# Refitting a list scheduler: measured latencies, GpSimd durations and the shared port, with new priorities

## The chip, the cores and the metric

The kernel runs on one core of a Trainium2 chip. The time is the device time of one execution in microseconds (us). The core has four engines that compute (PE, the TensorE that multiplies matrices; DVE, the VectorE; ACT, the ScalarE; POOL, the GpSimd) and SP, which issues most transfers. Each engine takes its instructions strictly in the order in which the program lists them: an instruction that waits holds up all that stand behind it on the same engine.

## The reference

Three layers follow each other. The first is a complex linear recurrence for 4 batches of 8 heads, 768 steps, head size 48; the second a gated feed-forward layer with a three-tap convolution over time; the third a causal attention with four experts, of which each token takes two. Cut to what matters:

```python
# layer 1: complex decay a (length limited to 0.999), state S, output y
for t in range(S):
    S_re, S_im = ar * S_re - ai * S_im + kv, ar * S_im + ai * S_re   # kv = outer(k[t], v[t])
    y[:, :, t] = einsum('bhd,bhde->bhe', q[:, :, t], S_re)
# layer 2
h = maximum(x @ w_in, 0); conv = sum_k conv_w[k] * shift(h, k)
x = (h * sigmoid(conv)) @ w_out
# layer 3, for each of 4 experts e
a = softmax(causal((x @ wq[e]) @ (x @ wk[e]).T / 8))
out += gate[e] * (a @ (x @ wv[e])) @ wo[e]                           # gate: the two best of x @ w_gate
```

## The kernel before

Stage 1 replaces the recurrence by sums over chunks of 128 steps. The decays are turned to logarithm and angle (`polar`, `phase` in `e_ops`, with Ln, Exp, Arctan and Sin on ACT and elementwise work on DVE), summed along time by a matmul with a triangle (L437), and multiplied onto q and k (`rotate`; the products go through `Ctx.mul`, L394). `e_ops` does this for 12 units of 256 tokens, three to a batch. `m_ops` then does 24 chunks of 128 tokens: the scores of a chunk (PE L585), their causal mask (DVE L587), the state (PE L605, DVE L614), the output (PE L623 and L627), its copy to SBUF (ACT L633) and, for each unit, a store to the buffer `x_scr` in DRAM.

Stage 2 (`s2_ops`) takes 8 blocks of 384 tokens. A block loads its `x` from `x_scr`, splits it into a rounded part and a rest (`Ctx.cp`, a cast, L384 on ACT or L386 on DVE; then a subtraction, L394), multiplies by `w_in` (PE L762, nine matmuls a slice of 128 features), applies Relu (ACT L773), the convolution (DVE L784, 16 of them a block), Tanh (ACT L786) and the gate (DVE L787), and multiplies by `w_out` (PE L800). The weights are unpacked on the way from 64-bit words (`weights`, L684 to L694). Stage 3 (`s3_ops`) is the attention: projections (PE L870, L920), scores (PE L1017, L1018; DVE L1026; ACT L1029), transposes (PE L1042), the product with v (L977) and the last projection (L998), then the store to `out`.

None of this is written in the order in which it runs. Every step is entered in a list with what it reads and writes, the engines that may do it (`alts`: an engine and an assumed duration for each) and a priority. `Sched.run` then plays a list scheduler: it goes through assumed time, gives each free engine the ready step of the smallest priority number, chooses between engines by who would end first, places the tiles in memory, and `emit` writes the instructions in the order of assumed start times. So assumed durations and latencies decide the order of instructions, which engine takes a step, and nothing else: the program still waits for real data by semaphores. Three things in the model are touched by the change:

- Latencies: `Sched.LAT` is what passes from the end of a step to the start of one that needs it on another engine.
- The port that DVE and POOL share: a step is in `lock` if it runs on POOL, or on DVE without touching PSUM and without `alone=True`; two locked steps never overlap in assumed time.
- Durations: `pool(n)` for an elementwise step of n columns on POOL, `dve(n)` and `acts(n)` for DVE and ACT, and single numbers.

The dictionary `P` holds the offsets of all priorities, some buffer counts and thresholds. The assumed time of a transfer is not changed: it starts 0.65 us after its issue or when the one before it is through, moves 360 kB a microsecond, and is there 1.1 us later.

Where the scheduler foresees a gap on PE in the early part, it fills it with small matmuls on a constant tile (L641, `heat`, up to the first block of stage 2; L645, `warmth`, in foreseen gaps of over 0.6 us after that). They compute nothing that is used.

Of the kernel before, what the change touches and what calls it, by code (L numbers as in the profile page):

```python
# [14 lines left out]
AF = mybir.ActivationFunctionType  # L15
# [21 lines left out]
TWO_PI = 6.28318501  # L37
TINY64 = 1.125 * 2.0 ** -15
P = dict(tu=22.99, lag=1.78, tf=3.56, dn=29.40, pa=28.16, pf=31.65, pp=31.74, ps=19.16, pr=13.53, kn=9.56, pd=-10.31,
         py=-3.49, cw=7.07, cs=6.91, ne=3, sw=16.78, slack=0.33, hold=1.18, wl=0.23, bl=0.07, bc=0.37, hy=7.06,  # L40
         tb=28.68, xp=-21.85, jq=-1.43, jp=3.08, jv=-4.00, ja=-2.43, jf=16.61, jt=5.79, ju=0.10, jw=0.26, na=13, no=2,
         nt=6, ns=4, nx=7, nq=14, th=0.46, fr=0.20, nc=2, sd=1, ck=-587.37, up=61.76, big=0, a0=1, a1=4, u0=-0.59,
         u1=0.11, u2=3.11, u3=-0.41, u4=0.75, u5=1.55, u6=-0.26, u7=1.62, u8=0.57, u9=-4.01, u10=-7.57, u11=-0.52,
         v0=-0.57, v1=-0.88, v2=2.18, v3=0.15, v4=1.22, v5=1.18, v6=0.00, v7=-7.38, v8=-7.08, v9=-5.79, v10=3.04,
         v11=-7.00, b0=0.00, b1=-4.24, b2=-0.23, b3=7.87, b4=-0.60, b5=-0.53, b6=-3.32, b7=-1.95, b8=-2.61, c0=0.89,
         c1=-2.69, c2=1.81, c3=-0.52, pw=0.14, sp=1.00, jg=-4.92, pm=-1.39)
# [48 lines left out]
class Sched:  # L95
    LAT = {"PE": 0.32, "ACT": 0.2, "DVE": 0.2, "POOL": 0.22, "SP": 0.05}
# [63 lines left out]
    def run(self):  # L160
# [37 lines left out]
        while done < total:  # L198
# [95 lines left out]
            for s in o.out:  # L294
                s.nd -= 1
                lat = 0.06 if s.alts.keys() == {e} else self.LAT["SP" if "SP" in o.alts else e] + (0.22 if "PE" in s.alts else 0.0)
# [41 lines left out]
def acts(n):  # L338
    return 0.095 + n * 0.000834


def dve(n, fast=False):
    return 0.066 + n * (0.00052 if fast else 0.00104)


def pool(n):
    return 0.1 + n * 0.0019
# [56 lines left out]
def s1_ops(c):  # L404
# [10 lines left out]
    def e_ops(u):  # L415
# [23 lines left out]
        def polar(z, a, b):  # L439
# [16 lines left out]
                r=ks(im), w=ks(tmp), prio=pa, alone=True))  # L456
# [4 lines left out]
            S.op({"ACT": acts(N)}, lambda e: A.activation(g(tmp), g(re), AF.Exp, bias=c.cs["b_eps"], scale=-1.0),  # L461
# [14 lines left out]
        def phase(z, a, b):  # L476
# [44 lines left out]
            S.op({"ACT": acts(N)}, lambda e: A.activation(f(n), f(n), AF.Sin, scale=-TWO_PI, bias=c.cs["b_half"]),  # L521
# [46 lines left out]
    def m_ops(j):  # L568
# [60 lines left out]
        S.op({"PE": 2.07 if cc else 1.0}, f, r=[v, qp] + sm + ([s0] if cc else []), w=[ps], prio=d - P["py"])  # L629
# [41 lines left out]
def weights(c, src, cols, prio, early=False):  # L671
# [5 lines left out]
    else:  # L677
# [10 lines left out]
        S.op({"DVE": dve(cols, True), "POOL": pool(cols)}, lambda e: c.E[e].tensor_scalar(  # L688
# [571 lines left out]
```

## Time and profile before

| | us |
|---|---|
| median of 3 runs | 684.7 |
| lowest, highest run | 682.49, 687.74 |
| the profiled execution, its own time | 688.02 |
| its span, first to last instruction | 686.2 |
| PE, DVE, ACT, POOL busy | 643.2, 563.5, 482.9, 117.0 |
| mean granted TensorE clock | 0.989 of full speed |

The profiled execution is 3.3 us over the median of the runs. An engine is busy while one of its instructions runs, also when that instruction is held up inside by another engine. PEld is PE's loading of weights, which overlaps its matmuls. In the rows below, x26 is a number of instructions; behind a bar stand the busy time, the mean duration in ns, and the idle time of the engine before them with what ended it.

### The profile page before, as it was taken

To read this page: it belongs to the slowest core of one execution; us is meant where nothing else is said; L and a number is where in the kernel's file an instruction comes from. 1 tells how busy PE (TensorE), PEld (TensorE's weight loads), DVE (VectorE), ACT (ScalarE), POOL (GpSimd) and SP (SyncE) were. 2 spreads that over 40 slices of the span, in tenths; PEclk is the share of its full clock that TensorE was granted. 3 is DMA by queue.
4 is the path that set the end of the run, shared out by engine and by line. 5 is a ranking of instruction groups with operands and counts; after the bars stand their busy time and mean duration, and the time that the engine had idled before them with its cause. 6 is when DMAs were issued, how large, how long until landed. Compare 5 with 4: busy or idle time off the path is not lost. (4 is left out here: it accounts for less than half of the span.)

```text
span 686.2 us, 13132 instructions
## 1 busy us (share of the span) xinstructions
PE 643.2 (94%) x4724; PEld 574.3 (84%) x4724; DVE 563.5 (82%) x1235; ACT 482.9 (70%) x1007; POOL 117.0 (17%) x157
## 2 busy tenths in 40 slices
PE   6899698799999999999999999999989999999995
PEld 3568497799898899999999999996878889788874
DVE  5999799999989999989748998689687676876761
ACT  7968786788998977886427556469567745865762
POOL 0733120331242411102002000002111100100100
PEclk9999989999999999999999999999999999999998
DMA  8666857656647376455032231021011001000102
GB/s 310 162 201 187 229 155 219 189 174 205 169 158 222 102 225 188 128 154 162 24 114 83 71 105 57 1 70 36 1 36 69 36 1 68 4 1 1 47 25 75
DMA packets 54604, 76.58 MB, mean 112 GB/s; under 512 B 5104, under 2 KB 45936, under 8 KB 54528
## 3 DMA queue, kind: packets, MB, share of 16 engines
q1 hardware_dynamic: 54240, 75.04, 35.8%
q8 instruction: 39, 0.64, 0.4%
q0 software_dynamic: 288, 0.59, 0.3%
q14 instruction: 37, 0.30, 0.1%
HBM read 42.51 MB, written 14.16 MB: 83 GB/s over the span
## 5 line engine op out<-in xcount | busy, mean ns | idle before, releaser
L762 PE MATMUL banks<-arena_R 128*128 128x384 f32 (+1 forms) x472 | 103.8, 349 | 5.4 <-ACT arena_R L384 3.6
L800 PE MATMUL banks<-arena_R 128*128 128x384 f32 (+1 forms) x510 | 104.3, 344 | 0.0
L762 PEld LDWEIGHTS banks<-arena_R 128*128 128x128 f32 x472 | 84.8, 194 | 7.4 <-ACT arena_R L384 4.0
L800 PEld LDWEIGHTS banks<-arena_R 128*128 128x128 f32 x510 | 88.2, 188 | 2.0 <-issue 1.3
L384 ACT ACTIVATE arena_F<-banks 128x384 f32<-128x384 f32 (+4 forms) x146 | 61.4, 447 | 34.3 <-PE banks L1042 12.3
L784 DVE SCALAR_TENSOR_TENSOR arena_F<-arena_F 128x386 f32<-128x386 f32 (+1 forms) x128 | 77.6, 627 | 3.9 <-ACT arena_F L781 3.1
L384 ACT ACTIVATE arena_R<-arena_F 128x384 fp32r<-128x384 f32 (+2 forms) x85 | 44.6, 534 | 51.4 <-PE banks L800 20.6
L1029 ACT ACTIVATE arena_F<-arena_F 128x128 f32<-128x128 f32 (+5 forms) x96 | 63.5, 664 | 7.7 <-DVE arena_F L1026 7.0
L394 DVE TENSOR_TENSOR arena_R<-arena_F,arena_R 128x384 fp32r<-128x384 f32 (+1 forms) x86 | 56.6, 675 | 13.2 <-PE banks L800 10.0
L394 POOL TENSOR_TENSOR arena_F<-arena_F 128x768 f32<-128x768 f32 x26 | 50.5, 1946 | 93.4 <-issue 22.6
L1026 DVE CUSTOM_DVE_ANT_0 arena_F<-banks,cover 128x128 f32<-128x128 f32 (+5 forms) x96 | 56.9, 617 | 7.9 <-PE banks L1018 6.1
L394 DVE TENSOR_TENSOR arena_F<-arena_F 128x768 f32<-128x768 f32 (+1 forms) x65 | 60.9, 951 | 0.8 <-ACT arena_F L451 0.5
L358 ACT ACT_TABLE_LOAD x40 | 51.3, 1283 | 1.4 <-PEq L1252 0.8
L1042 PE MATMUL banks<-ident,arena_F 128*128 128x128 f32 x336 | 49.3, 275 | 2.5 <-DVE arena_F L386 2.1
L773 ACT ACTIVATE arena_F<-banks 128x384 f32<-128x384 f32 (+1 forms) x64 | 31.1, 487 | 25.7 <-PE banks L762 20.8
L1042 PEld LDWEIGHTS banks<-ident,arena_F 128*128 128x128 f32 x336 | 39.2, 141 | 7.7 <-DVE arena_F L386 2.5
L394 POOL TENSOR_TENSOR arena_R<-arena_F,arena_R 128x384 fp32r<-128x384 f32 (+1 forms) x18 | 20.2, 1122 | 127.8 <-ACT arena_R L384 120.0
L386 DVE COPY arena_F<-banks 128x512 f32<-128x512 f32 (+4 forms) x74 | 36.8, 517 | 4.4 <-PE banks L1042 2.1
L1017 PE MATMUL banks<-arena_R 128*128 128x384 f32 (+4 forms) x112 | 39.2, 359 | 1.2 <-ACT arena_F L384 1.0
L977 PE MATMUL banks<-arena_F 128*64 128x384 f32 (+2 forms) x288 | 39.7, 420 | 0.3 <-ACT arena_F L384 0.3
L787 DVE SCALAR_TENSOR_TENSOR arena_F<-arena_F 128x384 f32<-128x384 f32 (+1 forms) x64 | 36.2, 585 | 3.8 <-ACT arena_F L786 3.4
L623 PE MATMUL banks<-arena_Z 128*64 128x128 f32 x384 | 36.7, 278 | 0.8 <-ACT arena_R L384 0.8
(242 smaller groups left out, 1467.9 us busy)
## 6 DMA issues: line engine op xcount, KB each, us to landing
arena_F<-x_scr SPq DMA_DIRECT2D x12, 576.0 KB, 4.4
arena_Z<-v SPq DMA_DIRECT2D x12, 512.0 KB, 4.3
arena_C<-arena_F SPq DMA_DIRECT2D x36, 129.0 KB, 2.5
arena_F<-q SPq DMA_DIRECT2D x12, 384.0 KB, 4.0
arena_F<-k SPq DMA_DIRECT2D x12, 384.0 KB, 5.0
arena_B<-arena_F SPq DMA_DIRECT2D x36, 128.0 KB, 2.5
x_scr<-arena_Z SPq DMA_DIRECT2D x24, 192.0 KB, 3.3
out<-arena_F SPq DMA_DIRECT2D x24, 192.0 KB, 1.9
```

The costliest lines, as they stand in the source:

```text
L358: nc.scalar.preload_act_table_set(TABS[o.tab])
L384: self.A.activation(out(), in_(), AF.Copy)
L386: self.V.tensor_copy(out(), in_())
L394: self.E[e].tensor_tensor(out(), a(), b(), op=self.OPS[op])
L762: PE.matmul(ps.ap, wi[f][a][:, i * 128:(i + 1) * 128], x[i].ap, start=(n == 0), stop=(n == 8))
L784: S.op({"DVE": dve(no) + 0.06}, lambda e, i=i: V.scalar_tensor_tensor(cv.ap, h[:, i:i + no], cw[:, k3 + i:k3 + i + 1], cv.ap, op0=OP.mult, ...
L800: PE.matmul(o[:, i, :], a[:, m * 128:(m + 1) * 128], g_.ap, start=(f == 0 and n == 0 and len(g) == 1), stop=(f == FT - 1 and n == 2 and i ...
L977: PE.matmul(py[64 * r:64 * r + 64, :n], v[kb][:, o:o + HD], at[r][:, kb, :n], start=(kb == 0), stop=(kb == nk - 1))
L1017: PE.matmul(pp, q[:, qs], k[:, kk], start=True, stop=False)
L1026: S.op({"DVE": dve(n)}, lambda e: V.tensor_tensor_reduce(wide(a.ap), ps[:, :, :step], wide(c.cs["cover"][:, SEQ - n:]), 1.0, 3e38, op0=OP. ...
L1029: S.op({"ACT": acts(n) + 0.15}, lambda e: A.activation(a.ap, a.ap, AF.Exp, bias=nm.ap, scale=-1.0, accum_out=rs[:, at, r:r + 1]), r=[nm], ...
L1042: PE.transpose(pt[:, z, :], a[:, (g_ + z) * 128:(g_ + z + 1) * 128], ident)
```

## The change

No computation is added or dropped. The scheduler's model gets other numbers, and the priorities in `P` are fitted anew (41 of its entries differ; two lines stand for all). The minimum in `weights` (L688) may no longer run on POOL. The squares in `polar` (L454) are now counted as holding the shared port.

```diff
-P = dict(tu=22.99, lag=1.78, tf=3.56, dn=29.40, pa=28.16, pf=31.65, pp=31.74, ps=19.16, pr=13.53, kn=9.56, pd=-10.31,
+P = dict(tu=22.99, lag=1.78, tf=3.56, dn=28.53, pa=28.16, pf=31.65, pp=31.74, ps=19.16, pr=13.53, kn=10.80,
...
-    LAT = {"PE": 0.32, "ACT": 0.2, "DVE": 0.2, "POOL": 0.22, "SP": 0.05}
+    LAT = {"PE": 0.22, "ACT": 0.16, "DVE": 0.13, "POOL": 0.13, "SP": 0.05}
...
-                lat = 0.06 if s.alts.keys() == {e} else self.LAT["SP" if "SP" in o.alts else e] + (0.22 if "PE" in s.alts else 0.0)
+                lat = 0.0 if e == "PE" and "PE" in s.alts else self.LAT["SP" if "SP" in o.alts else e] + (0.1 if "PE" in s.alts else 0.0)
...
 def pool(n):
-    return 0.1 + n * 0.0019
+    return 0.19 + n * 0.00178 + (0.28 if n == 768 else 0.0)
...
                 g(tmp), g(im), g(im), 1.0, 0.0, op0=OP.mult, op1=OP.max, accum_out=okin[:, hi:hi + 1]),
-                r=ks(im), w=ks(tmp), prio=pa, alone=True))
+                r=ks(im), w=ks(tmp), prio=pa))
...
-            S.op({"ACT": acts(N)}, lambda e: A.activation(g(tmp), g(re), AF.Exp, bias=c.cs["b_eps"], scale=-1.0),
+            S.op({"ACT": acts(N) + 0.09}, lambda e: A.activation(g(tmp), g(re), AF.Exp, bias=c.cs["b_eps"], scale=-1.0),
...
-        S.op({"PE": 2.07 if cc else 1.0}, f, r=[v, qp] + sm + ([s0] if cc else []), w=[ps], prio=d - P["py"])
+        S.op({"PE": 1.9 if cc else 1.0}, f, r=[v, qp] + sm + ([s0] if cc else []), w=[ps], prio=d - P["py"])
...
-        S.op({"DVE": dve(cols, True), "POOL": pool(cols)}, lambda e: c.E[e].tensor_scalar(
+        S.op({"DVE": dve(cols, True)}, lambda e: V.tensor_scalar(
             t.ap.bitcast(F32), t.ap.bitcast(F32), TINY64, None, op0=OP.max), w=[t], prio=prio)
...
-        S.op({"PE": 0.66 * (nk - 2) + 0.69}, av, r=at + v[:nk], w=[py], prio=d + P["ja"])
+        S.op({"PE": 0.65 * (nk - 2) + 0.78}, av, r=at + v[:nk], w=[py], prio=d + P["ja"])
...
-        pd = 2 * (n // step) * (max(0.108, step / 2400) + 0.013)
+        pd = 2 * (n // step) * (max(0.108, step / 2400) + 0.013) + 0.06 * (nb - 1)
...
-        S.op({"ACT": acts(n) + 0.15}, lambda e: A.activation(
+        S.op({"ACT": acts(n) + 0.18}, lambda e: A.activation(
```

Line numbers of the changed kernel are one higher than those of the kernel before from L47 on (L394 is L395 there). The order is different nearly everywhere. Three places of it follow; `arena_F` and the like are the SBUF regions in which the tiles lie, `banks` is PSUM.

On POOL, its first work in stage 1, before:

```order
L688 TENSOR_SCALAR arena_F<-arena_F 128x384
L400 DMA arena_A_246<-arena_F 16x8x128 x2
L400 DMA arena_B_269<-arena_F 16x8x128 x3
L400 DMA arena_A_246<-arena_F 16x8x130 x2
L400 DMA arena_B_269<-arena_F 16x8x128 x2
L688 TENSOR_SCALAR arena_F<-arena_F 128x384 x3
L394 TENSOR_TENSOR arena_F<-arena_F 128x3x256
L688 TENSOR_SCALAR arena_F<-arena_F 128x384
L388 TENSOR_SCALAR arena_R<-arena_F 128x384
L394 TENSOR_TENSOR arena_Z_109<-arena_Z_109,arena_A_246 96x384
L394 TENSOR_TENSOR arena_F<-arena_F 128x768
L394 TENSOR_TENSOR arena_Z_109<-arena_Z_109,arena_C_449 96x384
```

The same place now:

```order
L401 DMA arena_A_253<-arena_F 16x8x128 x2
L401 DMA arena_B_276<-arena_F 16x8x128 x3
L401 DMA arena_A_253<-arena_F 16x8x130 x2
L401 DMA arena_B_276<-arena_F 16x8x128 x2
L389 TENSOR_SCALAR arena_R<-arena_F 128x384
L395 TENSOR_TENSOR arena_R<-arena_F,arena_R 128x384
L395 TENSOR_TENSOR arena_F<-arena_F 128x3x256
L395 TENSOR_TENSOR arena_F<-arena_F 128x768
L395 TENSOR_TENSOR arena_Z_109<-arena_Z_109,arena_C_454 96x384
```

The five L688 steps and most products of 96x384 (the state of a chunk times its decay) have left POOL for DVE. Over the whole program POOL loses 5 of 5 L688, 6 of 7 products of 96x384, 6 of 26 products of 128x768, and 6 of 19 subtractions of 384 and 386 columns; DVE issues 32 instructions more in all.

On SP, the transfers ahead of the first load of `x` (the row `arena_F<-x_scr`), before:

```order
L400 DMA arena_F<-w_in 128x768
L400 DMA arena_Z_109<-v 128x1024
L400 DMA arena_F<-a_im 128x768
L400 DMA x_scr<-arena_Z_109 48x4x256 x2
L400 DMA arena_F<-a_re 128x768
L400 DMA arena_F<-w_out 128x768
L400 DMA arena_F<-x_scr 128x3x384
L400 DMA arena_A_246<-arena_F 16x8x258 x6
L400 DMA arena_B_269<-arena_F 16x8x256 x6
```

The same place now:

```order
L401 DMA arena_F<-w_out 128x768
L401 DMA arena_F<-a_im 128x768
L401 DMA x_scr<-arena_Z_109 48x4x256 x2
L401 DMA arena_Z_109<-v 128x1024
L401 DMA arena_F<-x_scr 128x3x384
L401 DMA arena_F<-w_in 128x768
L401 DMA arena_F<-a_re 128x768
L401 DMA arena_A_253<-arena_F 16x8x258 x5
L401 DMA arena_F<-w_out 128x768
L401 DMA arena_A_253<-arena_F 16x8x258
```

One load instead of two stands between the store of the needed chunks and the load of `x`; three of the loads ahead of the store have gone behind.

On DVE, the last instructions ahead of the first cast of that `x`, before:

```order
L394 TENSOR_TENSOR arena_F<-arena_F 128x768
L394 TENSOR_TENSOR arena_R<-arena_F,arena_R 128x384
L394 TENSOR_TENSOR arena_F<-arena_F 128x3x256
L454 ISA arena_F,okin<-arena_F 128x768
L454 ISA okin 128x1
L447 TENSOR_SCALAR arena_F,okin<-arena_F 128x768
L394 TENSOR_TENSOR arena_F<-arena_F 128x768
L386 CAST arena_R<-arena_F 128x384
L394 TENSOR_TENSOR arena_R<-arena_F,arena_R 128x384 x3
```

The same place now:

```order
L460 SCALAR_TENSOR_TENSOR arena_F<-arena_F 128x768
L695 SCALAR_TENSOR_TENSOR arena_F<-arena_F 128x384
L395 TENSOR_TENSOR arena_Z_109<-arena_Z_109,arena_C_454 96x384
L387 CAST arena_R<-arena_F 128x384
L464 SCALAR_TENSOR_TENSOR arena_F<-arena_F 128x768
L395 TENSOR_TENSOR arena_R<-arena_F,arena_R 128x384
L395 TENSOR_TENSOR arena_F<-arena_F 128x768
L387 CAST arena_R<-arena_F 128x384 x2
L395 TENSOR_TENSOR arena_R<-arena_F,arena_R 128x384 x2
L387 CAST arena_R<-arena_F 128x384
```

All three casts of this `x` are now on DVE (before, two of them were on ACT). From the eighth L587, the mask of the last chunk that this `x` needs, to the first of these casts the program lists 26 rows on DVE before and 18 now. On PE, the L641 fillers go from 132 to 129 matmuls, the L645 fillers from 6 to 27; all other matmuls are the same in number. ACT has 42 table loads instead of 40.

## Rows read from the trace of the kernel before

**Rows 1.** The page: busy us and share of each engine.
```profile
PE 643.2 (94%) x4724; PEld 574.3 (84%) x4724; DVE 563.5 (82%) x1235; ACT 482.9 (70%) x1007; POOL 117.0 (17%) x157
```

**Rows 2.** Stretches: length, busy of PE, PEld, DVE, ACT, POOL, clock, DMA share, GB/s.
```profile
0.00:150.00 150.00, 127.04 (x1000) 101.41 (x1001) 133.44 (x276) 116.69 (x211) 42.17 (x44) 0.97 0.69 209
150.00:325.00 175.00, 170.50 (x1420) 163.18 (x1419) 164.77 (x282) 145.87 (x265) 41.56 (x54) 1.00 0.56 168
325.00:450.00 125.00, 124.74 (x806) 122.76 (x805) 100.26 (x191) 67.80 (x138) 9.07 (x33) 1.00 0.21 64
450.00:686.00 236.00, 220.95 (x1504) 186.94 (x1503) 165.04 (x489) 152.51 (x396) 24.24 (x26) 0.99 0.10 33
```

**Rows 3.** POOL's groups by line and shape, whole span.
```profile
L394 POOL TENSOR_TENSOR arena_F<-arena_F 128x768 f32<-128x768 f32 x26 | 50.5, 1946 | 93.4 <-issue 22.6 <-ACT arena_F L472 20.6 <-DVE arena_F L394 19.3
L688 POOL TENSOR_SCALAR arena_F<-arena_F 128x384 f32<-128x384 f32 x5 | 9.8, 1959 | 20.6 <-ACT arena_F L684 20.6
L394 POOL TENSOR_TENSOR arena_Z<-arena_Z,arena_C 96x384 f32<-96x384 f32 x4 | 3.7, 921 | 0.0
```

**Rows 4.** DVE's groups that read two SBUF tiles, 0 to 150 us.
```profile
L394 DVE TENSOR_TENSOR arena_F<-arena_F 128x768 f32<-128x768 f32 x22 | 24.5, 1125 | 0.0
L394 DVE TENSOR_TENSOR arena_R<-arena_F,arena_R 128x384 fp32r<-128x384 f32 x23 | 13.9, 620 | 0.2 <-ACT arena_R L384 0.2
L454 DVE CUSTOM_DVE_ANT_0 arena_F<-arena_F 128x768 f32<-128x768 f32 x6 | 7.4, 1234 | 0.0
```

**Rows 5.** The same kinds, 150 to 325 us.
```profile
L394 DVE TENSOR_TENSOR arena_F<-arena_F 128x768 f32<-128x768 f32 x29 | 28.8, 1005 | 0.5 <-ACT arena_F L451 0.5
L394 DVE TENSOR_TENSOR arena_R<-arena_F,arena_R 128x384 fp32r<-128x384 f32 x18 | 15.0, 853 | 0.1
L394 DVE TENSOR_TENSOR arena_R<-arena_F,arena_R 128x386 fp32r<-128x386 f32 x16 | 11.4, 719 | 2.2 <-PE banks L800 2.2
```

**Rows 6.** Single lines on DVE: shortest, median and longest of one, in ns.
```profile
L394 DVE TENSOR_TENSOR arena_R<-arena_F,arena_R x86: 540/552/2195, 20.7 to 670.5; 128x384 fp32r<-128x384 f32 x54, 128x386 fp32r<-128x386 f32 x30, 128x768 fp32r<-128x768 f32 x2
L394 DVE TENSOR_TENSOR arena_F<-arena_F x65: 539/947/2579, 5.1 to 314.4; 128x768 f32<-128x768 f32 x51, 128x384 f32<-128x384 f32 x14
L454 DVE CUSTOM_DVE_ANT_0 arena_F<-arena_F x13: 558/951/1996, 5.7 to 270.1; 128x768 f32<-128x768 f32 x11, 128x384 f32<-128x384 f32 x2
L587 DVE TENSOR_TENSOR arena_Z<-banks,tri x48: 669/680/693, 32.8 to 348.8; 128x512 f32<-128x512 f32 x48
L688 DVE TENSOR_SCALAR arena_F<-arena_F x12: 171/351/364, 15.0 to 149.4; 128x384 f32<-128x384 f32 x11, 128x24 f32<-128x24 f32 x1
```

**Rows 7.** SP in order of time: start us, us of issuing, transfer.
```profile
70.18 0.83 SPq L400 DMA_DIRECT2D x_scr<-arena_Z  x2
...
75.97 0.39 SPq L400 DMA_DIRECT2D arena_F<-x_scr  x1
```

**Rows 8.** DVE in order of time: start us, us, instruction, idle before.
```profile
64.56 0.68 DVE L587 TENSOR_TENSOR arena_Z<-banks,tri 128x512 f32<-128x512 f32 x1
...
79.00 1.69 DVE L394 TENSOR_TENSOR arena_F<-arena_F 128x768 f32<-128x768 f32 x1
84.69 0.36 DVE L386 CAST arena_R<-arena_F 128x384 fp32r<-128x384 f32 x1 [3.99 <-DMA arena_F<-x_scr]
```

**Rows 9.** ACT, the copy of the last chunk that the first block needs.
```profile
69.52 0.63 ACT L633 ACTIVATE arena_Z<-banks 128x512 f32<-128x512 f32 x1
```

**Rows 10.** The page's transfers: number, KB each, median us from issue to landing.
```profile
arena_F<-x_scr SPq DMA_DIRECT2D x12, 576.0 KB, 4.4
...
x_scr<-arena_Z SPq DMA_DIRECT2D x24, 192.0 KB, 3.3
```

**Rows 11.** PE alone in two stretches: busy us, granted clock, DMA share, GB/s.
```profile
82.00:92.00 10.00, 6.74 (x27) 0.66 0.58 129
136.00:144.00 8.00, 6.18 (x45) 0.79 1.00 311
```

**Rows 12.** DVE in order of time: the start of the fifth block's convolution.
```profile
316.21 1.27 DVE L784 SCALAR_TENSOR_TENSOR arena_F<-arena_F 128x384 f32<-128x384 f32 x2
```

More of the change, by code (lines that the diff above doesn't have):

```diff
@@ L38 @@
 TINY64 = 1.125 * 2.0 ** -15
-P = dict(tu=22.99, lag=1.78, tf=3.56, dn=29.40, pa=28.16, pf=31.65, pp=31.74, ps=19.16, pr=13.53, kn=9.56, pd=-10.31,
[L40 to L46, printed above, removed]
+P = dict(tu=22.99, lag=1.78, tf=3.56, dn=28.53, pa=28.16, pf=31.65, pp=31.74, ps=19.16, pr=13.53, kn=10.80,
+         pd=-10.31, py=-3.58, cw=7.07, cs=6.91, ne=3, sw=18.37, slack=0.33, hold=0.93, wl=0.23, bl=0.06,
+         bc=0.37, hy=8.95, tb=28.68, xp=-21.94, jq=-1.05, jp=3.17, jv=0.63, ja=1.91, jf=16.96, jt=4.48, ju=0.10,
+         jw=0.26, na=15, no=2, nt=6, ns=4, nx=9, nq=14, th=0.39, fr=0.20, nc=2, sd=1, ck=-584.75, up=61.76,
+         big=0, a0=3, a1=4, u0=-2.06, u1=0.11, u2=3.11, u3=-0.41, u4=0.75, u5=1.83, u6=-0.10, u7=1.62, u8=0.57,
+         u9=-4.01, u10=-7.21, u11=-0.08, v0=-0.43, v1=-0.88, v2=1.92, v3=0.15, v4=1.22, v5=1.55, v6=0.33,
+         v7=-7.48, v8=-9.19, v9=-11.52, v10=3.04, v11=-7.00, b0=-0.47, b1=-4.24, b2=-0.23, b3=7.87, b4=-0.55,
+         b5=-0.97, b6=-3.68, b7=-1.53, b8=-2.61, c0=0.72, c1=-2.89, c2=2.35, c3=-0.35, pw=0.14, sp=1.00,
+         jg=-4.92, pm=-1.39)
 TABS = {"E": "natural_log_exp_and_others", "T": "trig_and_small", "S": "sigmoid_and_others",
@@ L520, in phase @@
             S.op({"ACT": acts(N), "DVE": dve(N, True)}, mag, r=ks(w), w=ks(n), prio=pp_)
-            S.op({"ACT": acts(N)}, lambda e: A.activation(f(n), f(n), AF.Sin, scale=-TWO_PI, bias=c.cs["b_half"]),
+            S.op({"ACT": acts(N) + 0.09}, lambda e: A.activation(f(n), f(n), AF.Sin, scale=-TWO_PI, bias=c.cs["b_half"]),
                  w=ks(n), prio=psn, tab="TU", grp=u)
@@ L958, in group @@
              alone=True)
-        S.op({"DVE": 0.3, "POOL": 0.5}, lambda e: (V if e == "DVE" else G).tensor_copy(
+        S.op({"DVE": 0.3, "POOL": 0.51}, lambda e: (V if e == "DVE" else G).tensor_copy(
             gx.ap, gs[:, :, :, None].to_broadcast([128, 3, 2, HD])), r=[gs], w=[gx], prio=d + P["jg"])
```

## The prediction

> **What bounds the kernel now.** I read the page first. PE is busy for 643.2 of 686.2 us, DVE for 563.5, ACT for 482.9, POOL for 117.0 [rows 1]. Since that is an average over three stages, the busy time by stretches comes next [rows 2]. The reader is to see two regimes there. Up to 325 us DVE is nearly always busy (133.44 of 150, then 164.77 of 175) while PE in the first 150 us is busy for only 127.04, part of which are fillers. From 150 us on PE has hardly a gap: 170.50 of 175, 124.74 of 125, 220.95 of 236, and part of the last difference is the tail in which the last results are stored. PE's computing work is the same before and after. So the time can fall only as far as PE gets more of it done in the first 150 to 250 us, where DVE feeds it, or stands less later; a gain that DVE makes after that is lost on a full PE.
>
> Then I looked at what makes DVE slow where it bounds. The product of 128x768 takes 947 ns in the median but up to 2579, the subtraction 552 but up to 2195, and the squares of L454 951 but up to 1996; the mask L587, which reads PSUM, stays between 669 and 693 [rows 6]. The first three read two SBUF tiles, and are held up inside while POOL works. Last I looked at where all engines stand at once: the first load of `x`. DVE waits 3.99 us for it [rows 8], and around it the granted clock of PE is 0.66 in the mean over 10 us, that is part of it on the lower level of 1.2 GHz, after PE had stood; there is a second such dip, 0.79 over 8 us, at 136 to 144 us [rows 11].
>
> **The change, part by part.** The sum is made against the profiled execution's 688.0 us, 3.3 over the median of 684.7; I carry the difference over to the median unchanged.
>
> *POOL gives work to DVE.* The order moves 6 products of 128x768, 6 of 96x384 and 5 minima L688 to DVE. At 0.947, 0.55 (the median of the 384-column subtraction, the nearest row) and 0.351 us [rows 6] that is 5.7 + 3.3 + 1.8 = 10.8 us more on DVE; another 13 casts come from ACT, at 0.35 (the L688 row, as near in size) 4.6 us. The rest of what changes on DVE cancels within about 3. Where does it fall? I took each order up to the 65th L784, the first one of the fifth block, at 316.21 us in the trace [rows 12]: DVE lists 531 instructions ahead of it before, 529 now. So the 15 us lie behind it, where DVE is busy for 100.26 of 125 us under a full PE [rows 2]. Cost 0; if that cover were gone, 15 us.
>
> *What DVE gets back from the port.* Stretch, as mean less median times count: before 150 us 22 x 0.178 + 23 x 0.068 + 6 x 0.283 = 3.9 + 1.6 + 1.7 [rows 4, 6], from 150 to 325 us 29 x 0.058 + 18 x 0.301 + 16 x 0.167 = 1.7 + 5.4 + 2.7 [rows 5, 6]. Together 17.0 us. I count 41 port-holding POOL instructions up to there (26 products of 768 columns, 7 of 96x384, 5 L688, 3 others), so 0.41 us each. Seventeen of them leave: 7 us. For the 20 products that stay, the model's duration goes from 1.56 to 1.84 us, against 1.946 in the trace [rows 3], so it will put DVE's two-tile steps behind them rather than into them: at most 20 x 0.28 = 5.6 us, of which I take 2. Together 9 us on DVE before 316 us, bounds 0 and 17.
>
> By the Trainium skill, "SBUF — State Buffer", section "Who interferes with whom", the pair of ports is locked for a whole instruction and the loser is fully blocked. By that alone each POOL product could cost DVE its whole length, and 17 fewer would give back up to 33 us; the rows show 0.41 us each, since DVE had PSUM work to put beside most of them. The same section says that two SBUF inputs on DVE contend with POOL's reads, which agrees with L454's 1996 ns and with dropping its `alone`.
>
> *The first block's x.* The order puts one load, not two, between the store and the load of `x`; and 18 rows, not 26, on DVE between the last mask it needs and the first cast. In the trace the mask ends at 65.24, DVE has work until 80.69, and goes on at 84.69 [rows 8]. The 18 rows come to about two thirds of the 26 by medians, so 10.3 of these 15.5 us. The data need 19.4 us from mask to cast: 4.9 to the end of ACT's copy [rows 9], store issue at 70.18, load at 75.97 [rows 7], the rest landing. With median landings of 3.3 and 4.4 us [rows 10] it would be 12.6. So DVE's wait becomes 2.3 to 9.1 us instead of 4.0. The landing of 8.7 us here is twice the median and the transfers behind the load are of the same kind, so I take 8: 4 us more idle on DVE. But DVE and ACT come to this place with less done ahead of it, so stage 2 starts 2 to 5 us earlier, and what was not done is done beside it.
>
> So DVE is 9 - 4 = 5 us ahead by the fifth block, of which roughly 3 are gained while PE still has gaps. That is a term of **-3**, between 0 (all behind a full PE) and -13 (no wait grows).
>
> *PE's clock.* Lost at the lower level: 10 x 0.34 = 3.4 us and 8 x 0.21 = 1.7 us [rows 11]. The first dip follows the wait for `x`, which stays. At the second place there are now more L645 fillers; I take that dip as gone: **-1.7**, bounds 0 and -5.1. The 21 more fillers stand in foreseen gaps; where no gap is, each costs at most about what a matmul takes in such a stretch, 6.18 us / 45 = 0.14 [rows 11]: **+0.5**, at most 2.9.
>
> *Latencies and PE durations.* No instruction changes, only the order. PE stands for 4.5 + 0.3 + 15.1 us after 150 us [rows 2], of which the end tail is over a half and keeps its shape (in the order the last projections follow the last product with v, as before). Of the rest, some 9 us, I take **-2.5**; bounds 0 and -9. Two more table loads (1.3 us each) fall on ACT, which has 29 us free in 150 to 325: 0.
>
> Sum: -3 - 1.7 + 0.5 - 2.5 = -6.7, so 681.3 for the profiled execution and **678.0** for the median.
>
> **The rivals.**
> 1. *The port pays in full.* All 17 us of stretch go, no wait for `x` grows, both dips go: 684.7 - 17 - 5 = 663. For it: the model now has POOL's product within 6% of the trace, and the stretch sits where DVE bounds. Against: 20 products stay on POOL, and from 150 us on PE has only 4.5 us of gaps to give. Chance 0.2. It would also be what the lock rule of the Trainium skill leads to.
> 2. *Nothing to measure.* The order is another one, but PE is full from 150 us on, and what DVE gains ends in waits: 684.7, within 4. For it: [rows 2], and that the assumed time of transfers, which is what stands out in the trace, is not changed. Chance 0.2.
> 3. *Slower: waits for transfers take the place of the stretch.* The model still has a load there about 4 us after its issue (0.48 of issuing, 0.65, 590 kB at 360 kB a microsecond, 1.1), the first load of `x` took 8.7. Lists that are packed closer to the assumed landing, as DVE's 18 rows instead of 26, stand for the difference: 5 us more at the first block, 4 at each of the next two, less 3 that DVE gains by the port: 684.7 + 10 = 695. It decides once DVE's waits for `x_scr` loads sum to over 15 us (here 3.99 at the first), and PE then has its lower clock for two dips or more. Against: later blocks have a backlog of stage-1 work in front of them. Chance 0.15.
>
> **The numbers.** The forecast, 678 with its own range of 671 to 685, has 0.45. What I call measurable is 1%, 6.8 us, so faster is below 677.9 and slower above 691.5; the forecast lies on that border. Faster: half of the forecast's case and rival 1, 0.23 + 0.2, and the better half of rival 2's spread touches the border: 0.45. Slower: rival 3 without its milder part, 0.13. Same: 0.42. The range from 663 to 693 leaves out half of rival 1 and half of rival 3.
>
> **What would show it.** In the profile after: POOL busy at about 85 us with no L688, and DVE's products of 128x768 at a mean under 1.03 us (right for the port term); DVE's wait for the first `x` at 8 us and its cast before 84 us; no clock under 0.9 in any 8 us between 100 and 200; PE over 170 of 175 us from 150 to 325. Wrong: stretch as before, a second wait for `x_scr` of over 4 us on DVE, or PE with new gaps in the attention stage, of which I have costed only gaps that go.

## The result, and the profile after

The changed kernel is slower, by 0.5 to 0.8%. In the first measurement it took 690.98 us (median of 15 runs, 684.95 to 697.47) against 684.23 (682.08 to 688.17): ratio 1.0078, interval 1.0052 to 1.0104. In a second one it took 688.76 against 685.67: 1.0048, 1.0021 to 1.0075. The ratios leave out runs that are more than 1.5% above the fastest of their kernel, two of the 15 and one of the 12 in the second measurement. The forecast was 678.0: the time is above its own range of 671 to 685, inside the wide one of 663 to 693 and inside the 1% called no change, but the sign is wrong.

The profiled execution took 689.51 us, with a span of 687.7. Its line of the page, then its stretches (length, busy of PE, PEld, DVE, ACT, POOL, clock, DMA share, GB/s):

```profile
PE 649.3 (94%) x4736; PEld 577.9 (84%) x4742; DVE 563.9 (82%) x1267; ACT 480.4 (70%) x1005; POOL 84.5 (12%) x135
```

```profile
0.00:150.00 150.00, 130.29 (x970) 104.27 (x977) 129.84 (x285) 111.78 (x197) 28.34 (x37) 0.95 0.68 204
150.00:325.00 175.00, 171.64 (x1443) 163.15 (x1443) 163.90 (x295) 148.29 (x278) 31.61 (x45) 1.00 0.55 169
325.00:450.00 125.00, 123.58 (x816) 121.35 (x813) 101.26 (x192) 69.62 (x141) 7.79 (x33) 1.00 0.24 77
450.00:688.00 238.00, 223.78 (x1516) 189.16 (x1514) 168.92 (x498) 150.69 (x391) 16.73 (x20) 0.99 0.08 29
```

POOL fell to 84.5 us, as forecast. Beside the first row of [rows 2], the first row here misleads. DVE is busy for 3.6 us and ACT for 4.9 us less in these 150 us, but PE's clock is lower as well (0.95 for 0.97), and its 3.3 us more hold more fillers. A second trace of the same changed kernel (c_after, below), whose clock is 1.00 in this stretch, has

```profile
0.00:150.00 150.00, 130.37 (x1003) 102.28 (x1004) 133.89 (x289) 114.05 (x203) 28.45 (x39) 1.00 0.69 209
```

So DVE is busy about as long as before (133.44). What it was relieved of is in its groups, in the first trace, 0 to 150 us and then 150 to 325:

```profile
L395 DVE TENSOR_TENSOR arena_F<-arena_F 128x768 f32<-128x768 f32 x20 | 18.6, 954 | 2.0 <-ACT arena_Z L600 1.3 <-ACT arena_F L452 0.4 <-DVE arena_F L691 0.2
L395 DVE TENSOR_TENSOR arena_R<-arena_F,arena_R 128x384 fp32r<-128x384 f32 x23 | 12.6, 553 | 2.0 <-ACT arena_R L385 1.0 <-PE banks L801 1.0
L455 DVE CUSTOM_DVE_ANT_0 arena_F<-arena_F 128x768 f32<-128x768 f32 x5 | 4.8, 954 | 0.0
...
L395 DVE TENSOR_TENSOR arena_F<-arena_F 128x768 f32<-128x768 f32 x37 | 34.5, 950 | 0.3 <-PE banks L801 0.3
L395 DVE TENSOR_TENSOR arena_R<-arena_F,arena_R 128x386 fp32r<-128x386 f32 x18 | 10.0, 563 | 0.5 <-PE banks L801 0.5
L395 DVE TENSOR_TENSOR arena_R<-arena_F,arena_R 128x384 fp32r<-128x384 f32 x13 | 7.2, 551 | 0.4 <-PE banks L801 0.3
```

The means are now the medians of [rows 6]. By the prediction's own sum the stretch of these groups is 0.5 us where it was 17.0 [rows 4, 5].

What became of these 16.5 us can be counted. Of the 128x768 product there are 20 and 37 where there were 22 and 29: all six that POOL gave up are done before 325 us. Counted so for every kind of DVE instruction, at its median duration, DVE has 17.6 us more work in the whole program, and 12.2 of them come before 325 us. The kinds that are equally many in both kernels are no further: 203 us of them are done by 325 us before, 202 now, 204 in the second trace. So most of what the port gave back went into work that came from POOL and ACT. The rest went into idle time of DVE, 4.5 us more than before up to 325 us (1.3 in the second trace).

Some of that idle time is waiting for the weights. DVE and ACT, 50 to 150 us, before and then after (who waited, for whom, us in total, times, longest):

```profile
DVE arena_F L688 <- ACT arena_F L684: 0.9, 1, 0.9
...
ACT arena_F L684 <- DMA arena_F<-w_out: 1.5, 1, 1.5
ACT arena_F L684 <- DMA arena_F<-w_in: 1.4, 1, 1.4
```

```profile
DVE arena_F L689 <- ACT arena_F L685: 4.3, 4, 2.3
...
ACT arena_F L685 <- DMA arena_F<-w_out: 5.0, 2, 2.7
...
ACT arena_F L685 <- DMA arena_F<-w_in: 1.1, 1, 1.1
```

In the second trace DVE's wait is 2.9 us and ACT's for `w_out` 4.8.

The first load of `x` is the one place that went better than forecast. SP, then DVE (start, us, instruction, idle before):

```profile
64.54 0.84 SPq L401 DMA_DIRECT2D x_scr<-arena_Z  x2
...
69.70 0.41 SPq L401 DMA_DIRECT2D arena_F<-x_scr  x1
```

```profile
73.96 0.63 DVE L387 CAST arena_R<-arena_F 128x384 fp32r<-128x384 f32 x2 [1.78 <-DMA arena_F<-x_scr]
```

The load was there 4.3 us after its issue where it took 8.7 before [rows 7, 8], the cast came 10.7 us earlier, and DVE waited 1.8 us.

### The profile page after: what moved, and what is told of

It is laid out like the page before. It is cut to its first block, busy times and chain, and to the rows that moved or that the text cites. A ratio compares the mean times of both kernels' runs of the same rounds, so it can differ in the third digit from the quotient of the medians.

```text
span 687.7 us, 13173 instructions
## 1 busy us (share of the span) xinstructions
PE 649.3 (94%) x4736; PEld 577.9 (84%) x4742; DVE 563.9 (82%) x1267; ACT 480.4 (70%) x1005; POOL 84.5 (12%) x135
## 4 chain that ended last, share of the span: by engine, by line
PE 58%; DVE 17%; DMA 10%; ACT 7%; issue 4%; SPq 3%; POOL 0%; DVEq 0%; ACTq 0%; POOLq 0%
PE banks L801 11%; PE banks L763 11%; PE banks L978 5%; PE banks L921 4%; PE banks L1043 4%; PE banks L586 4%; PE banks L999 3%; PE banks L871 3%; DMA arena_F<-x_scr 3%; SPq L401 3%; DVE arena_F L395 2%; PE banks L624 2%; PE banks L1018 2%; PE banks L1019 2%; PE banks L438 2%
## 5 line engine op out<-in xcount | busy, mean ns | idle before, releaser
L763 PE MATMUL banks<-arena_R 128*128 128x386 f32 (+1 forms) x520 | 108.6, 347 | 5.9 <-ACT arena_Z L600 2.3
L801 PE MATMUL banks<-arena_R 128*128 128x384 f32 (+1 forms) x513 | 101.2, 342 | 0.0
L763 PEld LDWEIGHTS banks<-arena_R 128*128 128x128 f32 x520 | 92.0, 191 | 9.2 <-ACT arena_Z L600 2.4
L801 PEld LDWEIGHTS banks<-arena_R 128*128 128x128 f32 x513 | 89.1, 189 | 1.1 <-issue 0.4
L785 DVE SCALAR_TENSOR_TENSOR arena_F<-arena_F 128x384 f32<-128x384 f32 (+1 forms) x128 | 81.6, 656 | 3.4 <-ACT arena_F L782 2.9
L385 ACT ACTIVATE arena_R<-arena_F 128x384 fp32r<-128x384 f32 (+2 forms) x78 | 41.4, 541 | 43.8 <-PE banks L801 14.4
L395 DVE TENSOR_TENSOR arena_R<-arena_F,arena_R 128x384 fp32r<-128x384 f32 (+2 forms) x92 | 52.8, 582 | 16.6 <-PE banks L801 10.5
L395 DVE TENSOR_TENSOR arena_F<-arena_F 128x768 f32<-128x768 f32 (+1 forms) x71 | 60.4, 874 | 2.8 <-ACT arena_Z L600 1.3
L395 POOL TENSOR_TENSOR arena_F<-arena_F 128x768 f32<-128x768 f32 x20 | 39.2, 1965 | 76.9 <-DMA arena_F<-k 12.2
L787 ACT ACTIVATE arena_F<-arena_F 128x386 f32<-128x386 f32 (+1 forms) x64 | 32.1, 523 | 13.0 <-DVE arena_F L785 12.9
L921 PE MATMUL banks<-arena_R,arena_Z 128*128 128x384 f32 x192 | 37.8, 343 | 1.0 <-DVE arena_R L935 0.7
L788 DVE SCALAR_TENSOR_TENSOR arena_F<-arena_F 128x386 f32<-128x386 f32 (+1 forms) x64 | 35.8, 578 | 2.3 <-ACT arena_F L787 1.8
```

Of the source, the lines that this page charges most:

```text
L385: self.A.activation(out(), in_(), AF.Copy)
L395: self.E[e].tensor_tensor(out(), a(), b(), op=self.OPS[op])
L763: PE.matmul(ps.ap, wi[f][a][:, i * 128:(i + 1) * 128], x[i].ap, start=(n == 0), stop=(n == 8))
L785: S.op({"DVE": dve(no) + 0.06}, lambda e, i=i: V.scalar_tensor_tensor(cv.ap, h[:, i:i + no], cw[:, k3 + i:k3 + i + 1], cv.ap, op0=OP.mult, ...
L801: PE.matmul(o[:, i, :], a[:, m * 128:(m + 1) * 128], g_.ap, start=(f == 0 and n == 0 and len(g) == 1), stop=(f == FT - 1 and n == 2 and i ...
L921: PE.matmul(ps.ap, wt[a][:, o:o + 128], y[:, i, :], start=(z == 0), stop=(z == 8))
```

## The experiments

An *order* below is one list of instructions per engine, as the scheduler leaves it. A plan's end is the last assumed time in that scheduler's own arithmetic, no time of the chip. The theories by their letters: A, the clock makes the difference; B, the new priorities (or numbers) carry it by themselves; C, waits for transfers; P, the port costs what the model says; E, the port is overpriced; W, the weight loads; D, many small waits; F, a fitted order has luck that others lack; G, the loss lies in fitting to exact landings and an exact port; H, the plan's end decides; M, the new numbers make worse orders under any fit.

**The clock and the fillers.** The changed kernel without, and with more, L646 fillers; and the changed kernel itself again.

```diff
-                if gap > 0.6 and own:
+                if False and own:                                          # e3_no_warmth
+                if gap > (0.25 if y.start < 160 else 0.6) and own:         # e4_more_warmth
-                    n = int(0.85 * (y.start - at) / 0.215)
+                    n = int((1.7 if y.start < 160 else 0.85) * (y.start - at) / 0.215)   # e4_more_warmth
```

> The changed kernel without its 27 L645 fillers (they compute nothing that is used). Theory A: PE falls to its lower clock at least once more between 80 and 145 us, mean clock at or below 0.982, 692 to 697 us. Theories B and C: the fillers only take PE slots, so without them 687 to 691 us, at an unchanged clock.

> The changed kernel with 62 instead of 27 L645 fillers: in the first 160 us of assumed time every foreseen gap of PE over 0.25 us is filled twice over. Theory A: the dips between 80 and 145 us go or shrink, mean clock 0.990 or more, 682 to 687 us, and the spread between runs falls. Theories B and C: 35 more matmuls of 0.14 to 0.22 us on a PE that bounds, 692 to 698 us.

> The changed kernel itself, unaltered, as the measure for the runs beside it and for a second trace of it: 688 to 693 by every theory.

Measured: e3 691.1 us, ratio to the kernel before 1.0078 (1.0034 to 1.0121); e4 691.1, 1.0089 (1.0054 to 1.0124). Both are as the changed kernel, just outside what theory A wanted for e3 (692 to 697) and far from it for e4 (682 to 687), so more fillers bring no time and the clock theory fails. They do bring clock: its mean over the runs is 0.981 in e3, 0.988 in the changed kernel and 0.989 in e4. By the slope given below that is about 4 us between e3 and e4, so the fillers take about as much as they give back. The repeat shows why the theory looked right. PE alone in three stretches (us, busy, clock, DMA share, GB/s) in the first trace of the changed kernel, then in the second:

```profile
90.00:100.00 10.00, 10.00 (x80) 0.66 0.25 90
110.00:118.00 8.00, 7.40 (x70) 0.79 0.97 276
144.00:152.00 8.00, 7.62 (x39) 0.79 0.62 216
```

```profile
core 0: 682.6 us, clock 0.998
...
90.00:100.00 10.00, 8.53 (x93) 1.00 0.35 118
110.00:118.00 8.00, 7.63 (x83) 1.00 0.95 279
144.00:152.00 8.00, 8.00 (x60) 1.00 0.32 111
```

The same program, one execution with three falls to the 1.2 GHz level, one with none in these stretches; their spans are 687.7 and 682.6. The first loses 10 x 0.34 + 2 x 8 x 0.21 = 6.8 us of full clock there, and the spans are 5.1 apart. So a fall seen in one trace need not belong to the order. The order has a share in the mean all the same: it is 0.981 in e3, and 0.978 and 0.980 in n2 and e2 below. Over all runs that tell their clock (115 of the kernel before, 27 of the changed one) time goes with the mean granted clock, by 513 and 521 us for a whole unit (least squares), and at full clock the two kernels stand at 679.5 and 683.6 us (679.5 and 684.3 without the slowest one and three of them). Such a slope is not the price of the clock alone, since an execution in which PE stands more can also fall more. The mean clocks of the two are 0.9882 and 0.9877, which is 0.3 us. The clock makes one kernel's runs differ; it does not make these two kernels differ. The Trainium skill, "TensorE: Matmul & The Clock Gate", Part 1, says of the slow matmuls at a kernel's start that their number differs from run to run; these traces show the like in mid-kernel, three falls and none. The page's figure of under 1% of a span is for that start; here, in mid-kernel, the two spans differ by 5.1 of 687.7 us.

**The two halves of the change.** The new model with the old `P`, and the old model with the new `P`.

```diff
-P = dict(tu=22.99, lag=1.78, tf=3.56, dn=28.53, ...
+P = dict(tu=22.99, lag=1.78, tf=3.56, dn=29.40, ...     # e1_old_prio: all of P, else the changed kernel
-    LAT = {"PE": 0.22, "ACT": 0.16, "DVE": 0.13, "POOL": 0.13, "SP": 0.05}
+    LAT = {"PE": 0.32, "ACT": 0.2, "DVE": 0.2, "POOL": 0.22, "SP": 0.05}   # e2_old_model: this and every other line of the change but P
```

> The change's model (latencies, durations, port) with the priorities of before. Theory A (the clock): the two orders feed PE equally well, and a kernel's time is about 681 us plus what PE loses at its lower clock; the changed kernel loses about 10 us that way (mean granted clock 0.985). Then this one's time follows its mean granted clock: 681 + 690 x (1 - clock), within 3 us, wherever it lands, and DVE's stretch by the port is as low as in the changed kernel (under 20 us against 34). Theory B (the priorities, fitted to the new model, are what is slower): this one is at 684 or below at the same clock as the changed kernel. Theory C (waits for transfers): 690 or more with DVE or ACT waiting over 10 us for x_scr loads.

> The old model with the new priorities. Theory A: again 681 + 690 x (1 - clock) within 3 us; DVE's stretch is back at about 30 us, which does not matter to the time by more than 2 us. Theory B: 690 or more whatever the clock. Theory C: as A, unless waits for x_scr loads sum to over 10 us.

Measured: e1 694.1 us, 1.0120 (1.0076 to 1.0164); e2 699.7, 1.0192 (1.0126 to 1.0257). By the medians each half alone is slower than the whole (e1 by 3 to 5 us, at the edge of what the intervals can tell, e2 by 9 to 11), so the loss is no sum of two parts: priorities are worth something only with the model they were fitted to. Theory B falls. Theory C does too: in e1's trace DVE and ACT together wait 5.1 us for loads of `x`, in e2's 1.1. Theory A's line gives 691.4 and 695.1 at their mean clocks of 0.985 and 0.980, within 3 us for e1 and 4.5 off for e2.

**The port.** Same order on every queue, POOL's products of 768 columns cut to a few; and the opposite, a model without any port. In p1 and p2 the kernel's own test of the range of the decays (L668, L669) is also set so that it never starts the slow second path, which cut products would call for. POOL's other instructions stay, and with them what they hold.

```diff
-            self.E[e].tensor_tensor(out(), a(), b(), op=self.OPS[op])
+            self.E[e].tensor_tensor(*((t[:, :, :8] if len(t.shape) == 3 else t[:, :24]) if e == "POOL" and n == 768 else t for t in (out(), a(), b())), op=self.OPS[op])   # p1, p2
...
-        o.lock = () if "SP" in alts or alone else tuple(
+        o.lock = () if True else tuple(        # r3_no_lock, with priorities searched anew
```

> The kernel before, with every instruction in its old place on every queue, but each product of 768 columns that runs on POOL (26 of them, 50.5 us of POOL) is cut to 16 or 24 columns, so nearly all holding of the shared port goes. It leaves out the rest of these products. Theory P (the port is worth what the new model says, it was only masked by the new order): the 25 us of DVE stretch before 325 us go and the time falls by 8 us or more, to 677 or less. Theory E (the port is overpriced: PE sets the end and DVE puts PSUM work beside POOL's products): 681 to 685, a gain of under 4 us, although DVE's busy time falls by 15 us or more.

> The same cut in the changed kernel (20 products of 768 columns on POOL), same order otherwise; it leaves out the same part. Theory P: little is left to gain, 689 to 691, so that p1 ends 12 us or more below this one. Theory E: 688 to 691; the gap between the two orders without any port stays at 4 to 8 us, that is, the order is slower by itself and not through the port.

> The numbers of the changed kernel, but the shared port taken out of the model altogether (no step is ever locked), with priorities searched for that: its plan ends at 634.8 us of assumed time, and POOL gets far more work. Theory E (the port is overpriced and could be left out of the model): 675 to 682. Theory P (a POOL product holds DVE for much of its length, about 0.3 us or more on the path for each, as the cut products showed): the 12 us of the plan go into stretch, 690 to 705, with DVE's products of 768 columns at a mean above 1.2 us.

Measured: p1 675.8 us, 0.9857 (0.9809 to 0.9905); p2 686.7, 1.0006 (0.9975 to 1.0036), both against the kernel before; r3 763.7, 1.1136. Theory E falls, with r3 altogether; of its sentences one holds, that the order is slower by itself. The cut takes 9.8 us (6.5 to 13.1) off the old order and 3 to 5 off the new one (its ratio of 1.0048 to 1.0078 less 1.0006, uncertain by some 3 us); it also gives POOL's results sooner, so these are upper bounds for the port. By them the change saved about 6 us at the port (2 to 10). But theory P's other half falls as well: with these products cut in both, the new order is 10 us slower (1.0006 / 0.9857; 6 to 14 from the two intervals together). About 8 of these are left at equal clock, since the mean clock is 0.990 in p1's four runs and 0.986 in p2's ten. "Order" includes here which engine does a step: p1 leaves out 26 products and p2 only 20, as DVE does the other six in full (5.7 us), and the rest of DVE's 17.6 us more is in p2 alone, too. How much of the 10 us is this work, and how much the sequence, the two runs do not separate. Stretches of p1, then of p2:

```profile
0.00:150.00 150.00, 130.64 (x1026) 104.60 (x1027) 132.73 (x285) 120.40 (x217) 30.90 (x51) 0.98 0.70 209
150.00:325.00 175.00, 174.84 (x1488) 169.58 (x1488) 155.32 (x289) 146.73 (x273) 14.12 (x49) 1.00 0.58 168
```

```profile
0.00:150.00 150.00, 129.10 (x962) 102.91 (x963) 125.34 (x280) 109.69 (x194) 15.02 (x37) 0.95 0.69 204
150.00:325.00 175.00, 173.17 (x1452) 165.07 (x1452) 159.91 (x299) 150.19 (x281) 17.03 (x45) 1.00 0.55 168
```

With the port out of the way DVE is busy for 7.4 and ACT for 10.7 us more in the old order's first 150 us than in the new one's, and PE then for 174.84 of 175. A part of that is the clock of these two executions, 0.98 and 0.95. The loss is there by 325 us: without the fillers (138 and 156, all before 150 us) PE has about 2376 matmuls behind it in p1 and 2258 in p2. r3, whose priorities are others again, shows what a port left out of the plan does: 242.2 us of POOL (before 117.0), and its DVE (first a line that reads two SBUF tiles, then the mask that reads PSUM) and POOL:

```profile
L785 DVE SCALAR_TENSOR_TENSOR arena_F<-arena_F 128x386 f32<-128x386 f32 x64 | 52.8, 830 | 9.6 <-ACT arena_F L782 8.5
L588 DVE TENSOR_TENSOR arena_Z<-banks,tri 128x512 f32<-128x512 f32 x48 | 32.1, 680 | 5.8 <-PE banks L586 5.8
...
L395 POOL TENSOR_TENSOR arena_F<-arena_F 128x768 f32<-128x768 f32 x49 | 99.6, 2035 | 58.9 <-ACT arena_F L452 20.3 <-ACT arena_F L471 12.0 <-ACT arena_F L522 8.4
```

The convolution step, 612 ns in the median undisturbed, takes 830; the mask stays at 680. The Trainium skill, "SBUF — State Buffer", section "Who interferes with whom", says that DVE contends with GpSimd's reads where it has two SBUF inputs; which line is stretched and which isn't agrees. The loss, 78 us, is far more than theory P wanted; its mean clock, 0.951, is part of it.

Why the fit chose the new order can be argued from the model's own arithmetic, in assumed time, each order kept as it is: with the new numbers the old order ends at 659.0 and the new one at 649.1; with the lock taken out, at 644.8 and 648.4. So the model charges the old order 14 us for the port and the new one 1, where the chip had at most 9.8 and 3 to 5, and it gives 3.6 us of everything else for that. With the lock out and the old latencies put back, the same arithmetic gives 647.3 and 657.4: longer latencies make the new order 10 us worse than the old one. That is a lead to what the chip's 10 us are, and no run follows it up. All this is the model's side only; the chip shows the two prices and the 10 us.

**The late weight loads.** Of the last four of the 16 loads of `w_in` and `w_out`, two of each, only 24 kB are fetched, in the same order. (The two expectations say eight; the edit starts at the thirteenth.)

```diff
-        c.load(lambda: raw.ap.rearrange("p a b -> p (a b)"), lambda: src.bitcast(U32), 1024 * cols, [raw], prio)
+        m = 48 if cols == DM and len(c.converted) >= 12 else 2 * cols; c.load(lambda: raw.ap.rearrange("p a b -> p (a b)")[:, slice(0, m)], lambda: src.bitcast(U32)[:, slice(0, m)], 1024 * cols, [raw], prio)
```

> The changed kernel in its own order, but of the last eight of the sixteen 384 kB loads of w_in and w_out only 24 kB are fetched (the rest of those weights is left out). In the changed kernel ACT L685 waits 5.0 us between 50 and 150 us for such loads and DVE L689 behind it 4.3 us; in the kernel before 2.9 and 0.9. Theory W (the minimum L688 moved from POOL, which could wait, to DVE, which cannot, and DVE now stands for the weights): 684 to 688, 3 to 6 us less than the changed kernel. Theory D (the loss is spread over many small waits of the order, and no single transfer carries it): 689 to 692.

> The same cut of the last eight loads of w_in and w_out in the kernel before, in its own order; the rest of those weights is left out. Theory W: 683 to 686, at most 1.5 us less, since the waiting is done by POOL there. Theory D: 682 to 686 as well; a fall as large as in the changed kernel would say that it is the traffic and not the waiting on DVE.

Measured: w1 687.6 us, 1.0032 (1.0002 to 1.0062); w2 684.3, 0.9996 (0.9962 to 1.0030). ACT's and DVE's waits of w1, 50 to 150 us:

```profile
ACT arena_F L685 <- DMA arena_F<-w_out: 2.8, 1, 2.8
...
DVE arena_F L689 <- ACT arena_F L685: 2.1, 3, 1.4
```

The wait that is left, at 109 us, stands behind a load that is fetched in full (2.7 us at 106 us in the changed kernel); of those behind the cut loads, 1.1 us at 130 and 2.3 at 143 us there, none is left. The changed kernel gains 1 to 3 us (1.0048 to 1.0078 less 1.0032), no more than its two measurements differ. 687.6 lies in theory W's range, but the gain is under the 3 to 6 us that the theory wanted; w2's time fits both. So the last four loads carry at most 3 of the 10 us, and this is not clear of noise. What the four before them carry was not tried, so between theories W and D nothing is settled.

**Neighbours and other fits.** Two orders in which one latency of the model is moved by 0.01 us, and four further sets of priorities.

```diff
-    LAT = {"PE": 0.32, "ACT": 0.2, "DVE": 0.2, "POOL": 0.22, "SP": 0.05}
+    LAT = {"PE": 0.31, "ACT": 0.2, "DVE": 0.2, "POOL": 0.22, "SP": 0.05}     # n1, else the kernel before
-    LAT = {"PE": 0.22, "ACT": 0.16, "DVE": 0.13, "POOL": 0.13, "SP": 0.05}
+    LAT = {"PE": 0.22, "ACT": 0.16, "DVE": 0.14, "POOL": 0.13, "SP": 0.05}   # n2, else the changed kernel
-P = dict(tu=22.99, lag=1.78, ...
+P = dict(tu=22.99, lag=1.76, ...     # r1; another set each in r2, r4, r5
```

> The kernel before with a single number of its model changed by nothing that a trace could tell: the latency behind PE 0.31 instead of 0.32 us. Priorities and all else as before. Theory F (the old order is the best of many that were fitted, and any other order, the changed kernel's too, lacks this luck): 689 to 696, as slow as the change with its two halves. Theory B (the new numbers or the new priorities carry the loss): 683 to 687, since neither is in it.

> The changed kernel with one latency of its model, that behind DVE, 0.14 instead of 0.13 us, which reorders as many instructions as n1 did. Theory F (a fitted order has luck that any nudge destroys): 694 or more. If the changed kernel has no such luck to lose: 688 to 693.

> The model of the kernel before, word for word, with a third set of priorities, searched for a plan that ends early also if transfers land 0.5 to 1.5 us later than assumed and if the port holds DVE only for the rest of a POOL instruction; its plan ends at 643.6 us of assumed time (before 646.5, after 649.1). Theory G (the loss is the fit: the new priorities were fitted to a plan in which the port locks out whatever stands beside it): 676 to 682, since a fit to a looser port and later transfers ends earlier. Theory F (the old fit was a lucky one, and any new fit ends higher): 688 to 695.

> A second order near that of r1 (old model, priorities searched on for another hour of the same kind): by theory G again 680 to 685; above 688 would say that r1 was luck.

> The model of the changed kernel, word for word (lock, durations, latencies), with priorities searched further for the earliest end of its own plan alone: 646.5 us of assumed time, 2.6 less than the changed kernel's and as low as that of the kernel before. Theory H (the end of the plan is what counts, and the change was only fitted less far): 684 to 687. Theory G (a plan with a locking port is the wrong target): 688 to 694, little or nothing of the 2.6 arrives.

> The model of the changed kernel, word for word, with a fifth set of priorities, searched as r1 was (an early end also if transfers land 0.5 to 1.5 us later and if the port only holds DVE for the rest of a POOL instruction); its plan ends at 642.1 us, 7 less than the changed kernel's. Theory G (the new numbers are sound, what costs is priorities fitted to exact landings and to an exact port): 678 to 685, 6 us or more under the changed kernel. Theory M (the new numbers themselves make worse orders, whatever the fit): 688 to 694.

| kernel | model | priorities | plan's end | median us | ratio to before, interval |
|---|---|---|---|---|---|
| before | old | as given | 646.5 | 685.2 (115 runs) | 1 |
| n1 | old, 0.01 moved | same | 654.2 | 688.7 | 1.0041 (1.0008, 1.0074) |
| r1 | old | tolerant fit | 643.6 | 683.2 | 0.9978 (0.9945, 1.0010) |
| r5 | old | tolerant fit | 643.9 | 683.7 | 0.9970 (0.9943, 0.9996) |
| changed | new | as given | 649.1 | 689.8 (27 runs) | 1.0078, 1.0048 |
| n2 | new, 0.01 moved | same | 651.7 | 699.1 | 1.0214 (1.0179, 1.0250) |
| r2 | new | fitted on, to its own plan | 646.5 | 690.2 | 1.0071 (1.0038, 1.0104) |
| r4 | new | tolerant fit | 642.1 | 686.7 | 1.0022 (0.9993, 1.0051) |

What follows: a nudge that no trace could tell costs n1 3 us and n2 9 to 11, so each fitted order is better than the one neighbour that was tried, and the changed kernel has luck to lose as well. n2 lies where theory F wanted it; n1's 688.7 lies just under F's 689 to 696 and above B's 683 to 687. But the old fit was no lucky one that a new fit cannot reach: r1 and r5 (which was searched on from near r1) are 1.5 to 2 us *under* it, r1's interval reaching over 1, and theory F falls there. r1 is also above the 676 to 682 that theory G wanted. Theory H falls with r2, whose plan ends 2.6 us earlier and whose time is that of the changed kernel. r4 lies between theories G (678 to 685) and M (688 to 694) and settles neither: with the new model a tolerant fit takes some 3 us off (r2, which was searched further too, gained nothing), and with either kind of fit the new model stays 3 to 5 us above the old one. The plan's end ranks these kernels badly: r4 has the earliest and is not the fastest.

r5's interval puts it 0.04 to 0.57% under the kernel before, barely clear of it. Its first stretch:

```profile
0.00:150.00 150.00, 132.34 (x1030) 105.97 (x1031) 137.69 (x280) 120.12 (x208) 41.26 (x52) 0.98 0.70 206
```

DVE and ACT are busy there for 137.69 and 120.12 us, against 133.44 and 116.69 in the kernel before [rows 2], and 129.84 and 111.78 in the changed one (133.89 and 114.05 in its second trace).

## Why the prediction was wrong, step by step

- **What bounds.** Right. PE is full from 150 us on (171.64 of 175, forecast over 170), and DVE's time before that counts: p1 takes most of the holding away and wins 9.8 us.
- **POOL's work moved to DVE, 0.** Wrong in its place. I put some 15 us behind the fifth block because DVE lists as many instructions ahead of that block's first convolution as before. But that convolution itself has moved forward, from 316.21 us [rows 12] to

```profile
305.43 1.27 DVE L785 SCALAR_TENSOR_TENSOR arena_F<-arena_F 128x384 f32<-128x384 f32 x2
```

  while the work that both kernels share was no further by 325 us. So it marks nothing: 12.2 of the 17.6 us came before 325 us, and DVE's busy time after that grows only from 265.3 to 270.2 us. What this work costs in time is part of the 10 us below, and not separated. I also missed that POOL could wait beside everything and DVE cannot: L689 stands in DVE's queue for L685, which stands for a load; for the last four loads that is 1 to 3 us by w1, not secured.
- **The port, -3 of 9 us.** Right in sign, and too small on both counts: all 17 us of stretch in the groups that I added up went, and about 6 us of that arrived (p1, p2).
- **The first `x`, 4 us more wait.** Wrong in sign. The wait fell from 4.0 to 1.8 us, because the load took 4.3 us; I had carried its 8.7 over from one row into a wait of 8. The start of stage 2 moved by 10.7 us, not 2 to 5, and brought nothing: the mask of the ninth chunk came at 158.4 us, 146.8 before.
- **The clock, -1.7.** Wrong. I read two dips of one execution as a property of the order. Three came in the trace after, none in those places of its repeat, and the mean clocks of the two kernels are the same; the fair term was 0.
- **The fillers, +0.5.** Within what e3 and e4 can tell: they cost PE time and raise the clock by about as much.
- **Latencies and durations, -2.5, bounds 0 and -9.** This is the step that failed. I wrote that "no instruction changes, only the order", and let the order only gain. With POOL's 768-column products cut in both kernels the new order is 10 us slower (6 to 14; about 8 at equal clock), the moved work of the second item included. The step needed a bound on the bad side, and there was no row for it in one trace.

The sum as measured: about -6 for the port and +10 for the order is +4. The two are taken from the same four kernels and must add up to the difference, so this is no check of either. Rival 2 came nearest: it had the time unchanged within 4 us, where the ratios say 3.3 to 5.3 more, and it said that DVE's gain would not reach PE, though it gave waits as the reason and not the moved work. Rival 3 has the sign, but not by its mechanism: it wanted DVE to wait over 15 us for loads of `x`, and the trace has

```profile
DVE arena_R L387 <- DMA arena_F<-x_scr: 3.6, 3, 1.8
```

for the whole span. The waits behind the last four weight loads are of its kind and are at most 3 of its 10 us.

What stays open is what makes up the order's 10 us: the moved work, or waits, and which. No single group of DVE's or ACT's waits between 50 and 150 us is above 5.0 us in the trace. Why the new numbers, whose POOL product (1.84 us) is nearer to the traces, gave worse orders under two kinds of fit, is not shown either; there are only two orders of each, and r5 is near r1.

## What to carry to other kernels

Where a change lets a scheduler reorder everything, give the order a term of its own with bounds on both sides; here a nudge of 0.01 us in the model moved the time by 3 to 11 us, about as much as the resource that the change was about. When work moves between engines, count how much of it is done by a fixed time; a place in the list can move with the order. Price a resource by taking it out of both orders, queue by queue the same, and only then compare the orders. A model closer to the trace is not by itself a faster program: choose between fits on the chip. Fits that also hold when transfers land later were the better ones here (3 us with the new model, 1.5 to 2, at the edge of noise, with the old one).

## What the runs showed that was not expected

- The lower clock comes and goes between executions of one program: mean granted clocks of 0.986 and 0.998, and 5.1 us of span between them, are the same kernel. Between kernels the mean over the runs differs too: 0.981 without the L646 fillers, 0.989 with 62 of them, at the same time of 691.1 us.
- The first load of `x`, the same 576 kB, took 8.7 us in one order and 4.3 in the other.
- A plan without the shared port, the shortest of all on paper (634.8), was the slowest on the chip (763.7).
